# Two DMA queues for the first block's loads, and an earlier place for tile 3's statistics, in a transformer layer kernel

## The chip, the cores and the metric

The kernel runs on one core of a Trainium2 chip. Its time is the device time in microseconds (us) of one execution; the time before is the median of four runs. The core has a matrix engine (TensorE, PE in the profile), a vector engine (VectorE, DVE), an engine for activation functions (ScalarE, ACT), a general one (GpSimd, POOL) and one that mostly issues transfers (SyncE, SP). All data comes from and goes to the chip's main memory by DMA.

## The reference

A transformer layer on 2048 tokens with 1024 features: x plus attention of the normalised x, then that plus a dense part of its own normalised value.

```python
def _layernorm(x, axis=-1, eps=1e-5):
    m = jnp.mean(x, axis=axis, keepdims=True)
    v = jnp.var(x, axis=axis, keepdims=True)
    return (x - m) / jnp.sqrt(v + eps)

# attention: 32 heads of 32, each token sees itself and the 255 tokens before it
qkv = (x @ wqkv).reshape(B, S, 3, H, Dh).transpose(2, 0, 3, 1, 4)
scores = jnp.einsum("bhqd,bhkd->bhqk", q, k) * (Dh ** -0.5)
p = softmax(where(mask, scores, -1e9))
o = jnp.einsum("bhqk,bhkd->bhqd", p, v).transpose(0, 2, 1, 3).reshape(B, S, D) @ wo

h = x + attention(_layernorm(x))
h2 = h + silu(_layernorm(h) @ w1) @ w2      # w1: 1024 x 3584, w2: 3584 x 1024
```

All inputs and the output are bfloat16.

## The kernel before

The tokens are cut into four blocks of 512, each into four tiles of 128 tokens (one per partition). For each block the kernel normalises the tiles, turns them so that features lie on the partitions (`lnT_b`), and multiplies them by wqkv: V for each tile and column half (`v_group`, eight matmuls over kt, the eight slices of 128 features), then Q and K (`qk_group`, line 250). The attention of a block runs between the matmuls of the next one. Then come the output projection and the dense part, also matmul after matmul. All instructions of an engine run in the order in which they are written in the source; nothing is rearranged.

The change lies in the opening: the loads of block 0, lines 151 to 157, and the treatment of its four tiles, lines 495 to 541. There the order is written out by hand so that PE can start early:

- SP issues all loads, one behind the other: x tile 0 (x0), x1, the left half of wqkv's V columns in four quarters of 256 KB (two kt slices each), x2, the right half of V in two pieces of 512 KB, x3, and the first 512 columns of Q (1 MB). The other Q and K columns are issued only after the transposes of the three tiles below. The completion of transfers is counted on eight semaphores used in turn, and an issue that reuses one waits until its earlier transfer has landed.
- Tiles 0 and 1 are not normalised before they are multiplied, only centred: `mean_first` takes their means (ACT, lines 459 and 462; DVE, 460 and 461), `center` subtracts them (DVE, 468 and 470), and `turn_first` turns them on PE (line 218), with a copy out of PSUM on ACT or DVE (line 219). `v_group(0, 0, 0)` and `v_group(0, 1, 0)` multiply them, and `scaled` multiplies the results by the reciprocal standard deviation, which comes later from `var_first` and `root_first` on ACT (lines 487 and 490) and `ln_recip` on DVE (line 212).
- ACT's queue starts with the load of its function table and a dummy activation (line 149), then L459 for tile 0 and L462 for tile 1, then the copies of tile 0's turns.
- Tile 2 gets its statistics on DVE (`ln_stats`, lines 174 and 182), its root on ACT (`ln_root`, line 209), its reciprocal and its normalisation on DVE (`ln_norm`, line 202). It is turned on PE between the matmuls of the right V half of tiles 0 and 1 (line 525); ACT copies the four pieces.
- Tile 3 gets the same statistics, root and normalisation, and is turned by a DMA transpose (`ln_transpose`, line 206) from SP. `norm_first` (line 493) normalises tiles 0 and 1 fully for Q and K; they too are turned by DMA transposes, behind tile 3's.
- PE then multiplies tile 2 and tile 3 by both V halves (lines 537 to 541), and the Q and K groups follow.

On DVE, the order after tile 2's normalisation is: `norm_first(0)`, tile 3's statistics, `norm_first(1)`, tile 3's reciprocal and normalisation. On ACT, tile 3's root stands behind all four copies of tile 2's turns; behind it are the two evictions of the right V half of tiles 0 and 1 (line 532).

Of the kernel before, what the change touches and what calls it, by code (L numbers as in the profile page):

```python
# [44 lines left out]
def kernel(  # L45
# [10 lines left out]
    nc = tc.nc  # L56
# [3 lines left out]
    S, D = x2d.shape  # L60
# [34 lines left out]
    def view(region, off, *dims):  # L95
        n = 1
        for d in dims:
            n *= d
        ap = region[:, off:off + n]
        if len(dims) == 2:  # L100
            return ap.rearrange("p (a b) -> p a b", b=dims[1])
        if len(dims) == 3:
            return ap.rearrange("p (a b c) -> p a b c", b=dims[1], c=dims[2])
        return ap
# [5 lines left out]
    x_ring = [view(r_o, i * 1024, 1024) for i in range(8)]  # L110
# [17 lines left out]
    wqkv_v = A_wqkv.rearrange("(kt p) n -> p kt n", p=P)  # L128
# [5 lines left out]
    def load_x(b, j, queue=nc.sync):  # L134
        queue.dma_start(out=x_ring[(b % 2) * 4 + j], in_=x2d[(b * 4 + j) * P:(b * 4 + j + 1) * P, :])

    def load_wqkv(c0, parts=1):
        dst = wqk[:, :, c0:c0 + 512] if c0 < 2 * D else wv[:, :, c0 - 2 * D:c0 - 2 * D + 512]
        n = KT // parts
        for k in range(0, KT, n):  # L140
            nc.sync.dma_start(out=dst[:, k:k + n, :], in_=wqkv_v[:, k:k + n, c0:c0 + 512])

    warm = view(r_e, 0, P)
    nc.vector.memset(warm, 0.0)
# [4 lines left out]
    nc.scalar.activation(out=dummy[:], in_=eps[:], func=ACT.Sqrt)  # L149

    load_x(0, 0)
    load_x(0, 1)
    load_wqkv(2 * D, 4)
    load_x(0, 2)
    load_wqkv(2 * D + 512, 2)
    load_x(0, 3)
    load_wqkv(0)

    ident = const.tile([P, P], BF16, name="ident")
# [13 lines left out]
    def ln_half(xt, stats, c):  # L173
        nc.vector.bn_stats(out=stats[:, c, :], in_=xt[:, c * 512:(c + 1) * 512])

    def ln_stats(xt, st, j, half_done=None):
        stats = half_done
        if stats is None:
            stats = small.tile([P, 2, 6], F32, name="ln_st", tag="ln_st")
            ln_half(xt, stats, 0)  # L180
        ln_half(xt, stats, 1)
        nc.vector.bn_aggr(out=st[:, j, :], in_=stats[:])
# [18 lines left out]
    def ln_norm(xt, st, rs, j):  # L201
        nc.vector.tensor_scalar(out=xt, in0=xt, scalar1=st[:, j, 0:1], scalar2=rs[:, j:j + 1],
                                op0=ALU.subtract, op1=ALU.mult)
# [4 lines left out]
    def ln_root(st, rs, j):  # L208
        nc.scalar.activation(out=rs[:, j:j + 1], in_=st[:, j, 1:2], func=ACT.Sqrt, bias=eps[:], scale=1.0)
# [4 lines left out]
    def turn_first(j, h, src, copy):  # L214

        for i in range(2):
            kt = h * 2 + i
            nc.tensor.transpose(out=tp_ps[h][:, i * P:(i + 1) * P], in_=src[:, kt * P:(kt + 1) * P], identity=ident[:])
        copy(out=lnT_b[0][:, h * 2:(h + 1) * 2, j * P:(j + 1) * P],
             in_=tp_ps[h][:, 0:256].rearrange("p (k q) -> p k q", q=P))  # L220

    def ln_tiles(tag):
        st = small.tile([P, 4, 2], F32, name=f"st_{tag}", tag=f"st_{tag}")
        rs = small.tile([P, 4], F32, name=f"rs_{tag}", tag=f"rs_{tag}")
        return st, rs
# [9 lines left out]
    def v_group(b, j, c, copy, between=None):  # L235
        acc = next_acc()
        for kt in range(KT):
            if between:
                between(kt)
            nc.tensor.matmul(acc, lhsT=lnT_b[b % 2][:, kt, j * P:(j + 1) * P], rhs=wv[:, kt, c * 512:(c + 1) * 512],  # L240
                             start=(kt == 0), stop=(kt == KT - 1))
        copy(out=v[:, b * 4 + j, c * 16:(c + 1) * 16, 0:DH], in_=acc.rearrange("p (h d) -> p h d", d=DH))
# [207 lines left out]
    st, rs = ln_tiles("a")  # L450
# [41 lines left out]
    def norm_first(j):  # L492
        nc.vector.tensor_scalar(out=x_ring[j], in0=x_ring[j], scalar1=mean[:, j + 2:j + 3], scalar2=rs[:, j:j + 1], op0=ALU.add, op1=ALU.mult)
# [18 lines left out]
    ln_recip(rs, 1)  # L512
    ln_recip(rs, 2)
    ln_norm(x_ring[2], st, rs, 2)
    norm_first(0)
    v_group(0, 1, 0, hold)
    scaled(0)
    scaled(1)
# [1 line left out]
    for k in range(0, KT, 4):  # L520
        for j in range(2):
            for kt in range(k, k + 4):
                if k and j:
                    turn_first(2, kt - k, x_ring[2], act)
                nc.tensor.matmul(pair[j], lhsT=lnT_b[0][:, kt, j * P:(j + 1) * P], rhs=wv[:, kt, 512:1024], start=(kt == 0), stop=(kt == KT - 1))  # L525
    ln_stats(x_ring[3], st, 3)
    ln_root(st, rs, 3)
    norm_first(1)
    ln_recip(rs, 3)
    ln_norm(x_ring[3], st, rs, 3)  # L530
# [43 lines left out]
    for g0 in range(0, G, 4):  # L574
        for w in range(2):
            for g in range(g0, g0 + 4):
                qk_group(0, w, g, dve if g % 2 else act)
                n = g0 * 2 + w * 4 + g % 4
# [181 lines left out]
```

## Time and profile before

| | |
|---|---|
| Runs | 692.54, 694.46, 694.34, 692.54 us |
| Median | 693.44 us |
| Profiled execution | 692.29 us, of which the span from the first to the last instruction is 690.5 us |
| PE busy | 685.8 us, 99% of the span |
| DVE, ACT, POOL busy | 290.0, 244.4, 160.4 us |
| Bytes moved | 61.48 MB, 89 GB/s in the mean over the span |
| Granted PE clock | 1.0 |

The profile follows one execution. A line of the timeline gives the start of an instruction (in us from the span's start), its length, its engine, its source line, what it writes and reads, and in brackets how long the engine had been idle and what ended that. The names are those of memory regions: r_o holds the x tiles, r_w the weights of Q, K and V and the turned tiles, tp, acc and o_ps are PSUM banks. PE's matmuls overlap by a part of their shown length, so the distance between two starts is what one costs. PEld is the loading of PE's weights, SPq the issuing of transfers by SP.

### The profile page before, as it was taken

The numbers are of one execution on the slowest core, as the hardware profiler recorded it, in microseconds if no ns is written. First come the engines' busy times: TensorE is split into PE (matmuls) and PEld (weight loads), VectorE is DVE, ScalarE is ACT, GpSimd is POOL, SyncE is SP. The second block draws the span as 40 slices with busy tenths as digits, with TensorE's granted clock in tenths as the row PEclk, the third lists the DMA queues.
The fourth block names the chain that finished last, engine by engine and source line by source line (L and its number), as shares of the span: only waits on it lengthen the run. The fifth ranks groups of instructions, "written<-read, shape, count | busy, mean of one in ns | idle before, by whom it ended". The sixth has DMA issues, their size and how long they took to land.

```text
span 690.5 us, 14241 instructions
## 1 busy us (share of the span) xinstructions
PE 685.8 (99%) x6011; PEld 331.3 (48%) x6011; DVE 290.0 (42%) x613; ACT 244.4 (35%) x464; POOL 160.4 (23%) x295
## 2 busy tenths in 40 slices
PE   9999999999999999999999999999999999999998
PEld 4444555555555555544444444444444444444445
DVE  5167646744444449533316133343133251333111
ACT  7226666666676666421310033300133100233000
POOL 1007666566666656500000000000000000000000
PEclk9999999999999999999999999999999999999999
DMA  7833141136240889971023310022300123100110
GB/s 246 286 51 82 40 97 44 26 64 184 72 131 17 246 231 285 220 267 52 11 85 111 87 39 0 1 91 70 85 0 1 21 92 94 39 1 1 30 39 24
DMA packets 78640, 61.48 MB, mean 89 GB/s; under 512 B 52464, under 2 KB 62704, under 8 KB 78576
## 3 DMA queue, kind: packets, MB, share of 16 engines
q1 hardware_dynamic: 78576, 60.57, 31.3%
q8 instruction: 47, 0.77, 0.5%
q14 instruction: 17, 0.14, 0.1%
HBM read 39.85 MB, written 8.39 MB: 70 GB/s over the span
## 4 chain that ended last, share of the span: by engine, by line
PE 98%; DMA 1%; ACT 0%; SPq 0%; DVE 0%; issue 0%
PE hacc L670 19%; PE hacc L707 18%; PE acc L250 17%; PE acc L707 11%; PE acc L670 9%; PE acc L271 7%; PE acc L240 7%; PE o_ps L383 5%; PE sc L303 3%; PE hacc L271 2%; PE sc L355 1%; DMA r_w<-in_A_wqkv_dram 1%; PE sc L329 1%; PE o_ps L240 1%; DMA r_w<-r_o 0%; PE o_ps L525 0%
## 5 line engine op out<-in xcount | busy, mean ns | idle before, releaser
L373 POOL TENSOR_SCALAR_AFFINE_SELECT r_e<-r_e 128x512 bf16<-128x512 bf16 (+1 forms) x288 | 157.4, 561 | 125.9 <-ACT r_e L363 61.9
L707 PEld LDWEIGHTS <-r_a 128*128 128x128 bf16 x952 | 90.9, 98 | 103.0
L670 PEld LDWEIGHTS <-r_w 128*128 128x128 bf16 x896 | 87.4, 98 | 105.0
L707 PE MATMUL hacc<-r_a 128*128 128x512 bf16 (+2 forms) x616 | 122.5, 360 | 0.0
L670 PE MATMUL hacc<-r_e,r_w 128*128 128x512 bf16 x456 | 100.9, 379 | 0.0
L315 ACT ACTIVATE r_e<-sc 128x768 bf16<-128x768 f32 x96 | 78.2, 814 | 48.0 <-PE sc L303 44.8
L679 ACT ACTIVATE r_n<-hacc 128x512 f32<-128x512 f32 x30 | 17.9, 597 | 178.9 <-PE hacc L670 178.9
L707 PE MATMUL acc<-r_a 128*128 128x512 bf16 x336 | 74.0, 379 | 0.0
L250 PEld LDWEIGHTS <-r_w 128*128 128x128 bf16 x512 | 44.2, 97 | 46.1 <-issue 1.0
L250 PE MATMUL acc<-r_t,r_w 128*128 128x512 bf16 x256 | 63.4, 379 | 0.0
L252 DVE CAST r_a<-acc 128x512 bf16<-128x512 f32 x56 | 38.6, 690 | 55.3 <-PE acc L250 55.0
L250 PE MATMUL acc<-r_w 128*128 128x512 bf16 x256 | 59.9, 379 | 0.0
L383 PEld LDWEIGHTS <-r_e 128*128 128x128 bf16 x1440 | 47.4, 96 | 17.9
L271 PE MATMUL acc<-r_o,r_a 128*128 128x512 bf16 x208 | 51.9, 379 | 0.0
L670 PE MATMUL acc<-r_e,r_w 128*128 128x512 bf16 x216 | 49.1, 379 | 0.0
L383 PE MATMUL o_ps<-r_a,r_e 128*128 128x33 bf16 x1440 | 48.1, 178 | 0.0
L722 DVE SCALAR_TENSOR_TENSOR r_t<-hacc,r_t 128x512 bf16<-128x512 f32 (+2 forms) x22 | 14.0, 635 | 57.0 <-PE hacc L707 57.0
L316 ACT ACTIVATE r_e<-sc 128x256 bf16<-128x256 f32 x96 | 37.6, 392 | 0.0
L722 DVE SCALAR_TENSOR_TENSOR r_t<-acc,r_t 128x512 bf16<-128x512 f32 x12 | 8.3, 691 | 64.2 <-PE acc L707 64.2
L680 DVE SCALAR_TENSOR_TENSOR r_a<-r_n,hacc 128x512 bf16<-128x512 f32 x30 | 20.6, 688 | 33.0 <-ACT r_n L679 33.0
L670 PE MATMUL hacc<-r_a,r_w 128*128 128x512 bf16 x144 | 32.9, 379 | 0.0
L271 PEld LDWEIGHTS <-r_a 128*128 128x128 bf16 x256 | 21.8, 97 | 22.3
(100 smaller groups left out, 540.3 us busy)
## 6 DMA issues: line engine op xcount, KB each, us to landing
r_w<-in_B_w_dram SPq DMA_DIRECT2D x8, 896.0 KB, 5.2
r_a<-in_B_w_dram SPq DMA_DIRECT2D x7, 1024.0 KB, 7.5
r_o<-in_A_x_dram SPq DMA_DIRECT2D x16, 256.0 KB, 4.1
r_w<-in_A_wqkv_dram SPq DMA_DIRECT2D x4, 1024.0 KB, 8.8
h_dram<-r_t SPq DMA_DIRECT2D x16, 256.0 KB, 3.1
r_t<-h_dram SPq DMA_DIRECT2D x16, 256.0 KB, 2.8
out_dram<-r_t SPq DMA_DIRECT2D x31, 128.0 KB, 1.7
r_e<-h_dram SPq DMA_DIRECT2D x3, 1024.0 KB, 5.6
```

The lines of the kernel that those rows point to most:

```text
L240: nc.tensor.matmul(acc, lhsT=lnT_b[b % 2][:, kt, j * P:(j + 1) * P], rhs=wv[:, kt, c * 512:(c + 1) * 512], start=(kt == 0), stop=(kt == KT ...
L250: nc.tensor.matmul(acc, lhsT=wqk[:, kt, col0:col0 + P], rhs=lnT_b[b % 2][:, kt, :], start=(kt == 0), stop=(kt == KT - 1))
L252: copy(out=(qT, kT)[which][b][:, g, :], in_=acc)
L271: nc.tensor.matmul(acc, lhsT=qT[b][:, g, j * P:(j + 1) * P], rhs=wo[:, g, c * 512:(c + 1) * 512], start=(g == 0), stop=(g == G - 1))
L303: nc.tensor.matmul(sc[hh // 2][half * 64:half * 64 + 64, hh % 2, col:col + qb - qa], lhsT=kT[t // 4][r0:r0 + DH, g, k0:k0 + 64], rhs=qT[b] ...
L315: nc.scalar.activation(out=tri[:, :, :, 64:256], in_=both, func=ACT.Exp, scale=scale)
L316: nc.scalar.activation(out=e[:, 1024:1280].rearrange("p (h q) -> p h q", q=P), in_=bank[:, :, 192:320], func=ACT.Exp, scale=scale)
L373: nc.gpsimd.affine_select(out=dst, in_=src, pattern=[[0, n] for n in dst.shape[1:-1]] + [[sgn, P]], compare_op=ALU.is_ge if upper else ALU ...
L383: nc.tensor.matmul(o_ps[pair][:, qt * 2 + hh, 0:VW], lhsT=chunk_of(i, bank, piece, pair, hh), rhs=v[:, b * 4 + kt, g * 4 + pair * 2 + hh, ...
L670: nc.tensor.matmul(acc, lhsT=w1[:, kt, ft * P:(ft + 1) * P], rhs=ln2T[b][:, kt, :], start=(kt == 0), stop=(kt == KT - 1))
L707: nc.tensor.matmul(acc[:, 0:c1 - c0], lhsT=gT[:, ft, j * P:(j + 1) * P], rhs=w2[ft // 4][:, ft % 4, c0:c1], start=(ft == 0), stop=(ft == F ...
L722: nc.vector.scalar_tensor_tensor(out=t_out[j % 2][:, c0:c1], in0=acc[:, 0:c1 - c0], scalar=0.5, in1=t_in[j % 2][:, c0:c1], op0=ALU.mult, o ...
```

## The change

The loads of block 0 are shared between two queues. x0, quarters 1 and 3 of the left V half, and everything behind them stay on SP; x1 and quarters 2 and 4 are issued by ACT, behind the dummy activation and ahead of L459. `load_wqkv` gets a list of queues, which its pieces take in turn.

In the treatment of the tiles, `norm_first(0)` moves from behind tile 2's normalisation to behind tile 3's statistics, just ahead of `norm_first(1)`. The statistics and the root of tile 3 are written inside the loop over the right V half, behind the first turn of tile 2. On ACT this puts tile 3's root behind the first of the four copies instead of behind the last.

```diff
-    def load_wqkv(c0, parts=1):
+    def load_wqkv(c0, parts=1, queues=(nc.sync,)):
...
         for k in range(0, KT, n):
-            nc.sync.dma_start(out=dst[:, k:k + n, :], in_=wqkv_v[:, k:k + n, c0:c0 + 512])
+            queues[k // n % len(queues)].dma_start(out=dst[:, k:k + n, :], in_=wqkv_v[:, k:k + n, c0:c0 + 512])
...
     load_x(0, 0)
-    load_x(0, 1)
-    load_wqkv(2 * D, 4)
+    load_x(0, 1, nc.scalar)
+    load_wqkv(2 * D, 4, (nc.sync, nc.scalar))
     load_x(0, 2)
     load_wqkv(2 * D + 512, 2)
     load_x(0, 3)
...
     ln_norm(x_ring[2], st, rs, 2)
-    norm_first(0)
     v_group(0, 1, 0, hold)
     scaled(0)
     scaled(1)
...
             for kt in range(k, k + 4):
                 if k and j:
                     turn_first(2, kt - k, x_ring[2], act)
+                    if kt == k:
+                        ln_stats(x_ring[3], st, 3)
+                        ln_root(st, rs, 3)
                 nc.tensor.matmul(pair[j], lhsT=lnT_b[0][:, kt, j * P:(j + 1) * P], rhs=wv[:, kt, 512:1024], start=(kt == 0), stop=(kt == KT - 1))
-    ln_stats(x_ring[3], st, 3)
-    ln_root(st, rs, 3)
+    norm_first(0)
     norm_first(1)
     ln_recip(rs, 3)
     ln_norm(x_ring[3], st, rs, 3)
```

## The prediction

> **What bounds the kernel now.** The page comes first: its busy lines, then its chain.
>
> ```profile
> span 690.5 us, 14241 instructions
> ...
> PE 685.8 (99%) x6011; PEld 331.3 (48%) x6011; DVE 290.0 (42%) x613; ACT 244.4 (35%) x464; POOL 160.4 (23%) x295
> ...
> PE 98%; DMA 1%; ACT 0%; SPq 0%; DVE 0%; issue 0%
> ```
>
> TensorE (PE) holds 98% of the chain. The change touches only block 0's opening, so what matters is when PE, working without a pause from then on, starts its last delayed stretch. The chain of waits, asked for the first 50 us, names that place (start, length, what):
>
> ```profile
> 1.73 0.43 SPq L141
> ...
> 2.20 4.51 DMA r_w<-in_A_wqkv_dram
> ...
> 6.75 0.38 PE acc L240
> ...
> 8.90 1.73 PE o_ps L240 x8
> ...
> 13.37 1.35 ACT r_w L219 x4
> 14.72 0.20 ACT rs_a L209
> ...
> 15.15 0.56 DVE r_o L202
> ...
> 15.72 2.84 DMA r_w<-r_o
> ...
> 18.61 1.90 PE o_ps L240 x8
> ...
> 22.23 27.63 PE acc L250 x128
> ```
>
> Two things are late: V quarter 2 (landing 6.71), and the transpose of tile 3, which PE's group at 18.61 waits for. The timeline of PE, and below it that of DVE, shows by how much (start, length, instruction; in brackets the idle time before and what ended it):
>
> ```profile
> 16.09 1.89 PE L240 MATMUL o_ps<-r_w 128*128 128x512 bf16 x8
> 18.61 1.90 PE L240 MATMUL o_ps<-r_w 128*128 128x512 bf16 x8 [0.63 <-DMA r_w<-r_o]
> ```
>
> ```profile
> 11.29 0.55 DVE L202 TENSOR_SCALAR r_o<-r_o,st_a,rs_a 128x1024 bf16<-128x1024 bf16 x1
> 11.76 0.54 DVE L493 TENSOR_SCALAR r_o<-r_o,mean,rs_a 128x1024 bf16<-128x1024 bf16 x1
> 12.21 1.28 DVE L174 BATCH_NORM_STATS2 ln_st<-r_o 128x6 f32<-128x512 bf16 x2
> ...
> 14.95 0.16 DVE L212 RECIPROCAL rs_a<-rs_a 128x1 f32<-128x1 f32 x1 [0.80 <-ACT rs_a L209]
> ```
>
> The group of 16.09 is free for its successor after 8 x 0.216 (1.73 / 8 in the chain), at 17.82. PE idles 0.79 there. This is all that an earlier tile 3 alone can win, and all that a later PE can lose for nothing.
>
> **When the loads land.** From the DMA view in narrow windows, issue start plus time to landing: x0 0.81 + 2.8 = 3.6; x1 1.26 + 2.8 = 4.1; V quarters 1 to 4: 5.8, 6.7, 7.4, 8.0; x2 3.73 + 4.9 = 8.6; second V half 10.2 and 11.5; x3 as in the row below, 5.27 + 6.9 = 12.2. So tile 3's statistics at 12.21 start on its landing, and the matmul of kt = 6 (timeline: 8.08) on quarter 4's.
>
> ```profile
> r_o<-in_A_x_dram SPq DMA_DIRECT2D x1, 256.0 KB, 6.9
> ```
>
> ```profile
> 5.00:6.00 1.00, 0.85 (x7) 0.52 (x8) 1.00 (x5) 1.00 (x4) 0.00 (x0) 1.00 0.91 282
> ...
> 11.00:12.00 1.00, 1.00 (x7) 0.41 (x5) 0.87 (x3) 1.00 (x3) 0.00 (x0) 1.00 1.06 382
> ```
>
> The two rows of stages (last columns DMA share and GB/s) say that the 16 DMA engines are full from the start on, so all transfers ahead of x3, the same 2.75 MB as before, take as long in two queues as in one.
>
> **Part 1, two queues.** Removed from SP: three issues of 0.43 to 0.51 each. They cover nothing late, since transfers wait in line rather than for SP. Added on ACT, behind the table load (0.80 to 2.08) and the dummy activation (2.10): three issues. No row shows an issue on ACT; SP's rows give 0.40 as the lower and 0.84 (x3's) as the upper end, so 1.2 to 2.5 together. I take 0.45 each, as nearly all SP rows have, so ACT is free at 2.2 + 1.35 = 3.55. ACT's first statistic (L459) waits for x0 until 3.58 anyway: cost nothing, but up to 1.1 at the upper end.
>
> SP now holds its later issues for other landings: x3's for quarter 1's (5.8), the first wqk load's for quarter 3's. Both cost nothing while the 1.25 MB ahead of them is on its way until 11.5; without that cover each costs its delay.
>
> x1 is issued at 2.2 instead of 1.26. Its landing is bounded by 2.2 + 2.8 = 5.0 (x0's and x1's time in an empty line) and 2.2 + 4.9 = 7.1 (x2's, five transfers ahead). With equal shares x1 runs beside quarter 1, and both are done when the same bytes were done before, up to 5.8; I take 5.4. ACT then runs L462 from 5.4 instead of 4.34, and the two copies (L219) behind it 1.06 later, so kt = 0 starts near 6.97, not 5.91.
>
> Quarter 2 runs beside quarter 3, so it lands with it at 7.4 instead of 6.7. Quarter 4 runs beside x2: 8.6 to 8.7 if they share equally; if x2's rows, twice as long, take two thirds, half of quarter 4 is left when x2 is done (about 8.2) and goes at half speed, 2 x 0.35 more: about 9.1 including landing. So kt = 6, which could start at 8.08, is late by d = 0.7 to 1.1. The late kt = 0 is hidden in this: from 6.97, four matmuls and two pairs of transposes (0.22 and 0.11 each) and one copy of 0.37 bring kt = 4 near 8.0, kt = 6 near 8.7. I take d = 0.9.
>
> d below zero is possible too: if ACT's queue is given its turn first, quarters 2 and 4 come as early as they could. Its upper end is x1 at 7.1: kt = 0 then starts at 8.6, d = 2.6.
>
> The Trainium skill ("DMA: Bandwidth & Descriptors", section "Issuing engines are not separate DMA queues") speaks against a gain: queues of different engines end in the same 16 DMA engines, and several issuers save issue time only. By it the sum would hold no faster loading at all; by the row of 5 to 6 us, which at 282 GB/s is below the later 382, a little room is left, and rival 1 prices it.
>
> **Part 2, the order on DVE and ACT.** norm_first(0) (0.45, start to start 11.76 to 12.21) moves behind tile 3's statistics. This frees DVE at 11.76, but x3 lands at 12.2: no gain where it left. It returns before the reciprocal: +0.45. ACT's root of tile 3 (L209) moves from behind four copies to behind the first. It waits for the statistics there, and three copies, then the two scaled evictions, queue behind it; PE's group of 14.36 reads these copies from kt = 2 on. The root ends near 14.0; the copies follow at 14.4, 14.7 and 15.1, each ahead of its reader (14.8, 15.2, 15.7): cost nothing, unless x3 is over 0.4 late.
>
> The 0.80 that DVE idled before the reciprocal goes. Statistics to end of norm_first(1) was 12.21 to 14.15, 1.94; plus 0.45 moved, plus 0.20 and 0.57 for reciprocal and norm: the transpose is issued at s + 3.16, where s is the start of the statistics. With s = 12.21 this is 15.37, 0.35 sooner than 15.72. But DVE reaches the statistics at 11.76 + d, since tile 1's copies and tile 2's statistics run behind PE.
>
> **The sum.** The end moves by the larger of two: PE, d - 0.79; tile 3, max(-0.35, d - 0.45 - 0.35) = max(-0.35, d - 0.80). For d = 0.9 this is +0.11. On the profiled execution: 692.29 (span 690.5 and 1.8 outside it) becomes 692.4. The median of the runs, 693.44, stands 1.15 above; the same shift gives 693.5. The order of the transposes and all work from 22.23 on stay, and PE has no idle there for a shift to enter.
>
> **A second cost, told apart.** The warm-up matmuls step by 0.425 (weight loads at 1.46, 1.88, 2.31 in the timeline), later ones by 0.216; after two short waits PE keeps the faster step. The Trainium skill ("TensorE: Matmul & The Clock Gate", Part 1) has the full clock granted after a busy window of about 3.4 us whose phase is not the kernel's; estimated from that page, one more window at half clock would add 1.7, where the rows above charge an early wait of PE only with its own length. No row here shows such a loss.
>
> **Rivals.** Rival 1, faster: a second queue fills the gaps of 4 to 6 us (293 and 282 GB/s against about 375 later). That is 2 x (375 - 288) / 375 = 0.46 earlier for x3 and the quarters. With the order's 0.35, tile 3 comes 0.81 sooner and PE's idle is used up: 692.6. For: DMA share 0.91 there. Against: the engines are full anyway.
>
> Rival 2, slower: ACT's queue starts late and then gets the lesser share. x1 lands at 7.1, ACT's statistic holds the copies behind it, and d = 2.6: +1.8, 695.3. With issues of 0.84 on ACT it is 1.1 more: 696.4. It decides from d = 0.8 on, and every us beyond is lost. For: x1 is issued 0.9 later and quarters 2 and 4 now share with x2, which nobody needs before 9.2. Against: the quarters were in line already behind x1.
>
> Rival 3, the loading changes nothing that PE sees, only the order on ACT and DVE counts: -0.35, 693.1.
>
> **How the numbers follow.** Forecast 0.45, rival 1 0.18, rival 2 0.25, rival 3 0.12. 0.3% is 2.08 us, about what a measurement of this kernel can tell from no change. The four times before lie in two pairs, 692.54 twice and 694.34 and 694.46, so a median can move by 1 either way without the change. Faster by over 2.08 takes more than rival 1: its gain, the lower pair, and early waits that I can't see: 0.13. Slower by over 2.08 is rival 2 at or above its centre, and the forecast on the upper pair with d over 1.9: 0.27. Same: 0.60. The range's low end is the lower pair less 0.35 and 0.79, 691.4; its high end is rival 2's upper price, 696.4. The forecast's own range is 692.4 to 694.6, one us around it.
>
> **What would show it.** Right: x1 landing 5.0 to 5.8, quarters 2 and 4 near 7.4 and 8.7 to 9.1, kt = 6 near 9; x3 still near 12.2; DVE without idle before the reciprocal of tile 3; its transpose issued at 15.6 to 15.9; PE's group of tile 3 at 18.5 to 18.9 with almost no idle before it. Wrong: x3 landing before 11.8 (rival 1), kt = 0 after 8 or PE at tile 3 after 20 (rival 2), a matmul step of 0.43 after 6 us, or a stretch behind 22 us that is longer than before.

## The result, and the profile after

The changed kernel takes 691.66 us (median of 30 runs); the kernel before, over 48 runs, 692.69. The ratio is 0.9984 with a 95% interval of 0.9979 to 0.9989: about 1.1 us faster, a small gain but clear of the noise. (Ratio and interval are taken from all runs, so the ratio differs a little from the quotient of the medians.) The forecast of 693.5, no change with a slight loss, had the sign wrong; its range held the time.

The page of the profiled execution (691.60) first: its span, its busy line and the queues.

```profile
span 689.9 us, 14241 instructions
...
PE 686.1 (99%) x6011; PEld 331.7 (48%) x6011; DVE 289.9 (42%) x613; ACT 244.2 (35%) x464; POOL 160.9 (23%) x295
...
q1 hardware_dynamic: 77888, 59.78, 31.1%
...
q10 hardware_dynamic: 688, 0.79, 0.3%
```

The span is 0.6 shorter. ACT's queue is q10; its 0.79 MB are x1 and two quarters. The chain of waits for the first 50 us (start, length, what):

```profile
0.81 2.87 DMA r_o<-in_A_x_dram
...
3.70 0.70 DVE ln_half L174
...
5.16 0.65 PE tp L218 x4
5.81 0.43 PE o_ps L167 x2
6.24 0.43 PE acc L240
...
9.11 1.73 PE o_ps L240 x8
...
14.74 1.73 PE acc L240 x8
16.46 3.45 PE o_ps L240 x16
19.92 1.73 PE acc L240 x8
21.64 27.63 PE acc L250 x128
```

Neither a V quarter nor a transpose stands in it any more. After x0's landing and the first statistics, PE alone makes up the chain from 5.16 on; tile 3's group is part of one run of 16 matmuls from 16.46. The long stretch of Q and K, 27.63 us in both kernels, starts at 21.64 instead of 22.23. These 0.59 are nearly the whole difference of the two spans. The timeline of ACT's issues, and below it DVE around tile 3, show where they come from.

```profile
0.80 1.28 ACT L149 ACT_TABLE_LOAD   x1 [0.80 <-PEq L745]
...
1.06 0.39 ACTq L135 DMA_DIRECT2D r_o<-in_A_x_dram  x1
...
1.49 0.96 ACTq L141 DMA_DIRECT2D r_w<-in_A_wqkv_dram  x2
...
2.09 0.20 ACT L149 ACTIVATE dummy<-eps 128x1 f32<-128x1 f32 x1
```

```profile
11.97 1.28 DVE L174 BATCH_NORM_STATS2 ln_st<-r_o 128x6 f32<-128x512 bf16 x2
13.28 0.21 DVE L182 BATCH_NORM_AGGREGATE st_a<-ln_st 128x2 f32<-128x12 f32 x1
13.41 0.95 DVE L493 TENSOR_SCALAR r_o<-r_o,mean,rs_a 128x1024 bf16<-128x1024 bf16 x2
14.27 0.15 DVE L212 RECIPROCAL rs_a<-rs_a 128x1 f32<-128x1 f32 x1
```

ACT issues x1 at 1.06, while its table load is still running and a full microsecond ahead of the dummy activation that stands before the issue in the program. So x1 is issued 0.2 earlier than on SP, not 0.9 later: "behind the dummy activation" holds for the order of the program, not for the time. The second thing is the rate of the loads, in the stages (last columns: DMA share, GB/s), first the stage of 4 to 5 us before the change, then two stages after it, and x3's row in the DMA view:

```profile
4.00:5.00 1.00, 0.96 (x3) 0.15 (x1) 0.85 (x4) 0.97 (x3) 0.00 (x0) 1.00 0.91 293
```

```profile
4.00:5.00 1.00, 1.00 (x3) 0.15 (x1) 0.85 (x3) 0.97 (x3) 0.00 (x0) 1.00 1.05 363
5.00:6.00 1.00, 0.92 (x7) 0.47 (x6) 1.00 (x6) 1.00 (x4) 0.00 (x0) 1.00 1.07 376
```

```profile
r_o<-in_A_x_dram SPq DMA_DIRECT2D x1, 256.0 KB, 6.2
```

Before, the two stages had 293 and 282 GB/s. x3 is issued at 4.97 and lands at 11.2 instead of 12.2, though the same bytes go ahead of it.

### The profile page after: what moved, and what is told of

Same layout as the page of the kernel before. It is cut to its first block, busy times and chain, and to the rows that moved or that the text cites. A ratio compares the mean times of both kernels' runs of the same rounds, so it can differ in the third digit from the quotient of the medians.

```text
span 689.9 us, 14241 instructions
## 1 busy us (share of the span) xinstructions
PE 686.1 (99%) x6011; PEld 331.7 (48%) x6011; DVE 289.9 (42%) x613; ACT 244.2 (35%) x464; POOL 160.9 (23%) x295
## 4 chain that ended last, share of the span: by engine, by line
PE 99%; DMA 0%; DVE 0%; issue 0%; DVEq 0%
PE hacc L671 19%; PE hacc L708 18%; PE acc L250 17%; PE acc L708 11%; PE acc L671 9%; PE acc L240 7%; PE acc L271 7%; PE o_ps L383 5%; PE sc L303 3%; PE hacc L271 2%; PE sc L355 1%; PE o_ps L240 1%; PE sc L329 1%; DMA r_o<-in_A_x_dram 0%; PE tp L218 0%; PE acc L527 0%
## 5 line engine op out<-in xcount | busy, mean ns | idle before, releaser
L671 PE MATMUL hacc<-r_a,r_w 128*128 128x512 bf16 x144 | 32.9, 379 | 0.0
```

The costliest lines, as they stand in the source:

```text
L671: nc.tensor.matmul(acc, lhsT=w1[:, kt, ft * P:(ft + 1) * P], rhs=ln2T[b][:, kt, :], start=(kt == 0), stop=(kt == KT - 1))
```

## The experiments

Ratios are against the kernel before on the same chip, where its median was 692.39 to 692.69; "Q starts" is the start of the long Q and K stretch in the chain of waits (or the end of the wait ahead of it), the place where everything in the opening is settled.

| Kernel | Ratio (95%) | Median us | x3 lands | Q starts |
|---|---|---|---|---|
| before, two profiles | 1 | 692.69 (48 runs) | 12.2, 12.3 | 22.23, 23.13 |
| changed, three profiles | 0.9984 (0.9979 to 0.9989) | 691.66 (30 runs) | 11.2, 11.3, 11.6 | 21.64, 22.13, 21.50 |
| e1, only the queues | 0.9992 (0.9983 to 1.0001) | 692.29 | 11.5 | 22.46 |
| e2, only the order | 0.9993 (0.9984 to 1.0002) | 692.24 | 12.7 | 22.35 |
| e3, all quarters on ACT | 1.0012 (1.0003 to 1.0021) | 693.48 | 11.9 | 23.47 |
| e4, x0 in two halves | 1.0024 (1.0013 to 1.0034) | 695.06 | 12.5 | 24.66 |
| e5, one queue, two halves of V | 1.0008 (0.9997 to 1.0018) | 692.78 | 12.1 | 22.16 |
| e6, ACT's issues late | 1.0091 (1.0077 to 1.0104) | 699.04 | 12.5 | 29.64 |
| e7, one filler less | 0.9986 (0.9977 to 0.9995) | 691.55 | 11.8 | 21.41 |
| e8, tile 0's transpose first | 0.9986 (0.9977 to 0.9995) | 691.79 | 11.7 | 22.27 |
| e9, weight loads wait | 0.9998 (0.9989 to 1.0007) | 692.24 | 11.8 | 22.14 |

**Each half alone.** e1 takes only the load part of the change, e2 only the order:

```diff
 e1: the order of before, and
-    load_x(0, 1)
-    load_wqkv(2 * D, 4)
+    load_x(0, 1, nc.scalar)
+    load_wqkv(2 * D, 4, (nc.sync, nc.scalar))
 e2: the order of the change, with the two lines above as before
```

> Only the loads are shared between the two queues; the order on DVE and ACT is that of before. Theory A (the loads land 1.0 sooner because the second queue fills gaps of the DMA engines, but tile 3's old place in the order hides it): x3 lands near 11.2, rate of 4 to 6 us above 350 GB/s, PE begins its groups without a wait for a quarter, but tile 3's root stands behind four copies, which end near 14.9, so its transpose is issued near 15.8 as before and PE idles 0.5 to 0.6 before tile 3; time -0.1 us against before (ratio 0.9998). Theory B (what counts is that PE no longer waits for quarters 2 and 4, the order is idle): -0.8 to -1.1, ratio 0.9985.

> Only the order on DVE and ACT is changed; all loads stay on SP. Theory A: x3 still lands at 12.2 and bounds the statistics; the transpose is issued 0.35 sooner, at 15.4, and PE's idle before tile 3 shrinks to about 0.4; time -0.35 us (ratio 0.9995), and the 4 to 6 us stages stay near 290 GB/s with single engines up to 1 us late in quarters 1 to 3. Theory B: no change of time. A rival on the gap: it was an accident of the one profiled execution; then x3 lands before 11.7 here too.

Each gives 0.3 to 0.6 us (0.33 and 0.38 by the medians against 692.62 on that chip, 0.55 and 0.48 by the ratios), with an interval that reaches no change. By the ratios the two add up to 1.03, nearly the 1.1 of the whole change, so the times don't show that the halves need each other; nor do they tell theory A from theory B in e1. The chain of e1, and then DVE's timeline of e2, say what each still waits for:

```profile
13.59 1.35 ACT r_w L219 x4
14.95 0.20 ACT rs_a L209
...
15.95 2.84 DMA r_w<-r_o
...
18.84 1.90 PE o_ps L240 x8
```

```profile
12.77 1.29 DVE L174 BATCH_NORM_STATS2 ln_st<-r_o 128x6 f32<-128x512 bf16 x2 [0.73 <-DMA r_o<-in_A_x_dram]
```

In e1, x3 is there at 11.5, but tile 3's root stands behind four copies, so the transpose is issued at 15.95 and PE idles 0.79 (its group before is free at 16.32 + 1.73 = 18.05). In e2 the order is ready and DVE idles 0.73 for x3, which lands 0.6 later than in before; so the transpose is issued at 15.85, not at the 15.4 that was expected. In these two profiles each half waits for what the other removes, as theory A had it. One detail failed: in e1, PE also waits until 8.3 for quarter 4. In both profiles Q starts later than in before (22.46 and 22.35 against 22.23), so the gain in their times isn't located.

**Does the matching matter?** e3 puts x0 and x1 on SP and all four quarters on ACT.

```diff
-    load_x(0, 1, nc.scalar)
-    load_wqkv(2 * D, 4, (nc.sync, nc.scalar))
+    load_x(0, 1)
+    load_wqkv(2 * D, 4, (nc.scalar,))
```

> As the changed kernel, but x0 and x1 stay on SP and all four quarters go on ACT's queue. Theory A (any second queue fills the gaps, the matching of the order is idle): x3 lands at 11.0 to 11.4, the rate of 4 to 6 us is above 350 GB/s, quarter 4 lands before 8.1; ratio within 0.0004 of the changed kernel's 0.9984. Rival (the matching order matters): quarter 4 lands after 8.3 since it shares with x2 and the second V half, PE waits at kt = 6, ratio 0.9990 or more.

The rival is right: slower than before by 0.8. PE waits 1.21 for quarter 4, which lands at 10.1 (timeline of PE):

```profile
10.12 0.38 PE L240 MATMUL acc<-r_w 128*128 128x512 bf16 x1 [1.21 <-DMA r_w<-in_A_wqkv_dram]
```

The rate is high here too (372 and 366 GB/s in the same stages): faster loading alone is no gain when a piece that PE needs comes late. ACT's fourth issue had to wait until 3.46 for the reuse of x0's completion semaphore; its bytes then moved beside those that SP had issued before. How much either adds was not tried.

**How much early ACT issues matter.** e6 builds what the forecast had assumed, and more: ACT's issues stand behind L459.

```diff
 (mean_first)
         nc.scalar.activation(..., accum_out=mean[:, 0:1])      # L459, waits for x0
+        load_x(0, 1, nc.scalar)
+        load_wqkv(2 * D, 4, (None, nc.scalar))                 # quarters 2 and 4
```

> As the changed kernel, but ACT's three issues stand behind the first statistic (L459), which waits for x0: x1 is issued near 3.8 instead of 1.06. This builds what the forecast had assumed, a late second queue. By the forecast's rule: x1 lands near 6.8, kt = 0 starts near 8.4, quarter 4 lands near 10, d = 2.0 to 2.5, so +1.2 to +1.7 us against before (ratio 1.0017 to 1.0025); with the clock falling back to half during PE's waits, as in the run with x0 in halves, another +1.5 (1.004). Rival (how early ACT issues does not matter, two queues are what counts): ratio 0.9990 or less.

It costs 6.3 us, far more than either expectation. The DMA view of 4 to 6 us shows a single queue, and the DMA row of x1 (issued at 3.54, so landed at 10.15) the result; the chain gives the same length:

```profile
q1 hardware_dynamic: 422, 0.51, 91.5%
```

```profile
3.54 6.61 DMA r_o<-in_A_x_dram
```

In the changed kernel both queues move bytes there (58.7% and 47.3% of the engines' time). In e6, ACT's queue moves nothing before 6, and has 5.8% from 6 to 7: what SP had issued earlier goes first. Nearly equal shares, which the forecast took, come at once where both queues start together; in e6 they come only from 8 on (46.9% for ACT's queue from 8 to 9, 58.6% for SP's). A part of the loss is PE's clock, granted at 0.50 from 8 to 16: from kt = 0 to the end of the next group of eight matmuls PE needs 7.1 us (11.70 to 18.83 in the chain), against 4.6 in the changed kernel (6.24 to 10.84).

**The landing of x0.** e4 loads x0 in two column halves, one on each queue; x1 follows on ACT.

```diff
-    load_x(0, 0)
+    nc.sync.dma_start(out=x_ring[0][:, 0:512], in_=x2d[0:P, 0:512])
+    nc.scalar.dma_start(out=x_ring[0][:, 512:1024], in_=x2d[0:P, 512:1024])
     load_x(0, 1, nc.scalar)
```

> As the changed kernel, but x0 is loaded in two column halves, one on each queue, ahead of all else. Theory A (in the changed kernel nothing but x0's landing and what follows it bounds PE, which never waits after 5.2): x0 lands 0.2 to 0.4 sooner, everything up to tile 3 moves with it; ratio 0.9980. Rival (the start is bound by PE's slow early clock, so earlier work is done at half speed): landing sooner, time as the changed kernel's, 0.9984.

Both expectations fail. The first turn starts 0.3 sooner (4.87), but x1 now lands at 5.2, ACT's statistic of tile 1 waits for it, and the copies of tile 0 wait behind that: kt = 0 starts at 6.76. Quarter 2 lands at 8.4. During these waits the clock drops (stages; the column before DMA share is the granted clock):

```profile
7.00:8.00 1.00, 0.48 (x4) 0.20 (x3) 0.42 (x3) 0.37 (x1) 0.00 (x0) 1.00 1.02 328
8.00:9.00 1.00, 0.56 (x3) 0.29 (x3) 0.00 (x0) 0.00 (x0) 0.00 (x0) 0.74 1.07 370
9.00:10.00 1.00, 1.00 (x7) 0.45 (x5) 0.00 (x0) 0.74 (x2) 0.00 (x0) 0.50 1.08 379
```

In the chain the matmuls of this stretch take 0.43 instead of 0.22. That is the loss which the prediction had told apart.

**One queue, larger pieces.** e5 keeps all loads on SP and cuts the left V half in two.

```diff
-    load_wqkv(2 * D, 4)
+    load_wqkv(2 * D, 2)          # with the order of the change
```

> All loads on SP, the left V half in two pieces of 512 KB instead of four quarters; order on DVE and ACT as in the changed kernel. Theory A (with one queue single DMA engines fall behind by 0.5 to 1 us wherever a transfer of 256 KB follows another, and never catch up): with fewer seams the last engine is late by less, x3 lands at 11.4 to 11.8, ratio 0.9988 to 0.9993 (kt = 0 waits for a half, landing near 6.5, which takes 0.3 back). Rival (one queue loses time whatever the size of its pieces): x3 lands at 12.2 or later, ratio 0.9995 or more.

x3 lands at 12.1, near the rival's 12.2 and about as late as with quarters. The second of the two pieces lands at 8.1 and PE waits for it. The rate is another matter (stages of e5):

```profile
4.00:5.00 1.00, 1.00 (x3) 0.15 (x1) 0.85 (x4) 0.97 (x3) 0.00 (x0) 1.00 1.04 360
5.00:6.00 1.00, 0.91 (x7) 0.44 (x7) 1.00 (x6) 1.00 (x4) 0.00 (x0) 1.00 1.01 331
```

One queue with larger pieces fills most of the gap of 4 to 6 us, and still brings x3 no sooner. A transfer has landed when the last of the 16 DMA engines has finished its part, and the trace's completion records show when each did. The first engine finished x3 at 10.8 in e5, 10.7 in the changed kernel and 11.2 in before; the last at 12.1, 11.2 and 12.2. So e5 has the rate but not the landing: some of its engines fall behind, as the expectations say of single ones. In the first profile of before, 15 of the 16 engines had finished quarter 1 at 4.9 and one at 5.9, and by quarter 3 the spread over the engines was 1.2 us. In the changed kernel's first profile the spread stays at 0.4 to 0.5 until quarter 3. In e7, with two queues, one engine is also 1.1 late, and x3 still lands at 11.8. Why an engine falls behind, and why two queues lose less by it, these runs don't show.

**Fillers and second profiles.** e7 leaves out one of the two short filler pairs. The runs called before_again, after_again and after_timed are the two kernels unchanged.

```diff
-    for i in range(2):
-        busy(2)
+    busy(2)
```

> As the changed kernel, but one of the two short filler matmul pairs that keep PE occupied before kt = 0 is left out (the fillers write nothing that is used). Theory A (PE bounds the opening from its first turn on, so what PE does there at half speed counts fully): kt = 0 starts 0.2 sooner, ratio 0.9981 to 0.9983. Rival (kt = 0 waits for ACT's copy, and less filling lifts PE's clock later): 0.9984 or more.

> The kernel before, for a second profile. If single engines fall behind at random in one queue, the engine that is late, and the landing of x3, differ from the first profile: x3 anywhere from 11.6 to 12.8, with a spread over the engines of about 1 us. If the gap were fixed, x3 lands at 12.2 again and quarter 1 lands at 5.8.

> The changed kernel, for a second profile. Theory A: x3 lands at 11.1 to 11.8 (three profiles with two queues so far), against 12.2 to 12.75 in four with one queue; stages of 4 to 6 us above 340 GB/s; PE reaches tile 3 without idle or with less than 0.2. If the first profile was lucky, x3 lands at 12 or later.

e7 is no different from the changed kernel. In its profile kt = 0 waited for quarter 1 until 6.2, so theory A is not tested there. The second profiles confirm x3's landing by queue: 12.1 to 12.7 in four with one queue, 11.2 to 11.9 in eight with two (the seven that follow the matching order, and e3). The other two with two queues, e4 and e6, have it at 12.5: a second queue alone does not bring it sooner. Quarter 4 is not safely sooner either: it lands at 7.6 to 8.6 in the seven, against 8.0 and 8.1 before. The second profiles also bring something else. Their Q stretches start late for a reason behind tile 3 (timeline of PE, before_again, then after_again):

```profile
23.13 2.10 PE L250 MATMUL acc<-r_w 128*128 128x512 bf16 x8 [0.83 <-DMA r_w<-r_o]
```

```profile
22.13 1.24 PE L250 MATMUL acc<-r_w 128*128 128x512 bf16 x5 [0.80 <-DMA r_w<-r_o]
```

The last of the three transposes, tile 1's, took 4.4 us there instead of 2.7, and the Q groups wait for it. Without that wait after_again would be the earliest of the changed kernel's three profiles, at 21.3.

**The slow last transpose.** e8 issues tile 0's transpose first; e9 holds the next weight loads back until the last transpose has landed.

```diff
 e8:
-    for j in (3, 0, 1):
+    for j in (0, 3, 1):
 e9:
+    fence = const.tile([P, 2], BF16, name="fence")
+    nc.sync.dma_start(out=fence[:], in_=lnT_b[0][:, KT - 1, P:P + 2])
     for c0 in (D, 512, D + 512):
         load_wqkv(c0)
```

> As the changed kernel, but SP issues the DMA transpose of tile 0 ahead of tile 3's (order 0, 3, 1 in place of 3, 0, 1); tile 0 is ready near 13.9, tile 3 near 15.0. Theory C (some executions lose 0.8 to 1 us because the last transpose runs beside the next weight load, as in the second profile of the kernel before, where it took 4.4 instead of 2.7): the last transpose is issued near 16.7 instead of 17.7 and lands near 19.5, two us before PE needs it; tile 3's is issued 0.2 to 0.3 later and lands near 18.2, so PE waits 0.1 to 0.2: median 691.6 to 691.9, and no execution above 692.3. Rival (those executions come from elsewhere): the same share, one in five, lies above 692.5.

> As the changed kernel, with one transfer of 512 bytes on SP behind the three transposes; it reads a corner of tile 1's turned data, so SP waits until the last transpose has landed (near 20.6) and issues the next weight loads behind it, 0.8 to 1.5 later than before (they are needed from 28 on, landing near 28; the transfer's result is not used). Theory C (the last transpose takes 4.4 instead of 2.7 in some executions, because the weight load behind it takes the DMA engines): the last transpose always lands near 20.6, no execution above 692.2, median 691.3 to 691.6; or +0.3 to +1 if the first of these loads now lands after PE needs it. Rival (the slow transpose is not caused by the load behind it): one execution in five above 692.4, as in the changed kernel.

> The changed kernel again, timed on the same chip as the kernel with the waiting loads, and a third profile of it. Ratio to before 0.998 to 0.999; two levels of time, near 691.6 and 692.5, the higher one where the last transpose takes 4.4 us. x3 lands at 11.1 to 11.8.

Neither beats the changed kernel, which on the same chip as e9 gave 691.46 (0.9987, 0.9979 to 0.9996) on two levels: seven of eleven runs at 691.33 to 691.49, three at 692.1 to 692.3. In e8, SP is busy with the issue of tile 0's transpose from 14.41 to 15.74, and tile 3's behind it is issued at 15.85 instead of 15.04; three of eleven runs still lie above 692.2. In e9 three of eleven lie 0.6 to 1.0 above the median, as without the wait, and in its profile the transposes took 3.1 to 3.4. So the load behind the transposes isn't shown to be the cause, and theory C is not supported.

The traces hold another candidate. In both profiles with the 4.4 us, a transfer of 16 KB that the profile lists as instructions (queue q8) starts while the last transpose is under way, at 19.6 in before_again and at 18.6 in after_again; then under 15 GB/s move from 20.4 to 21.7 and from 19.4 to 20.7. The DMA view of after_again from 17 to 19.5 has it:

```profile
q8 instruction: 1, 0.02, 3.9%
```

In the other twelve profiles it starts after the last transpose has landed, at 22.1 to 32.9, but for e8: there it starts at 19.6, when nearly all bytes of the transpose have moved. No run shifted this transfer, so it is not shown to be the cause. Nor is the slow transpose the only way to the upper level: the profiled execution of e8, at 692.24, belongs to it, and its transposes took 2.8. There PE waits for quarter 4 until 8.6 and again for tile 3.

## Why the prediction was wrong, step by step

**The rule of the sum held.** It said that the end moves by the larger of d - 0.79 (PE) and s + 3.16 - 15.72 (tile 3), d being the delay of kt = 6 and s the start of the statistics. The timeline of PE, before and then after, has the fillers, kt = 0 and kt = 6:

```profile
5.42 0.38 PE L167 MATMUL o_ps<-r_e 128*128 128x256 bf16 x2
5.91 0.38 PE L240 MATMUL acc<-r_w 128*128 128x512 bf16 x1
...
8.08 0.38 PE L240 MATMUL acc<-r_w 128*128 128x512 bf16 x1
```

```profile
5.60 0.63 PE L167 MATMUL o_ps<-r_e 128*128 128x256 bf16 x2
6.03 0.63 PE L240 MATMUL acc<-r_w 128*128 128x512 bf16 x1
...
8.29 0.38 PE L240 MATMUL acc<-r_w 128*128 128x512 bf16 x1
```

So d = 0.21, and s = 11.97. That gives -0.58 and -0.59; measured are -0.59 at the Q stretch and a transpose issued at 15.04, -0.68. In after_again and after_timed kt = 6 starts at 7.98 and 8.15, so the term of PE is -0.89 and -0.72; measured against 22.23 are -0.90, without the wait for tile 1's transpose, and -0.73. The inputs failed. The rule also divides the error of the forecast, +0.11, in this profile: d = 0.21 with x3 still at 12.2 gives -0.35, and the earlier x3 turns that into -0.58.

**First failing step: when ACT issues.** The prediction put the three issues behind the table load and the dummy, at 2.2. They ran from 1.06 to 2.45. With them, and with the higher rate, x1's landing was 4.3 (predicted 5.0 to 5.8), quarter 2's 5.7 (7.4), quarter 4's 7.6 (8.6 to 9.1), by issue plus time to landing. Quarter 4 had some luck in this profile: in e8, with the same loads, it landed at 8.6. Of each issue's length it was right: 0.39 to 0.5. The remaining d = 0.21 is not from loads, for PE waits for none; its slower step, 0.43 a matmul, lasted longer in this execution (the two fillers take 0.63 against 0.38 before, and kt = 0 takes 0.43 in the chain). The column of the granted clock reads 1.00 in both, so only the steps show this. In after_again, where kt = 0 takes 0.23, d is -0.10.

**Second failing step: "the engines are full".** It read the DMA share of 0.91 as full and forecast x3 at 12.2. The rows of 293 and 282 GB/s were a gap, which a second queue filled; e5 filled most of it in one queue, but with the last engine 1.4 us behind the first at x3. In the eight profiles with two queues and x3 at 11.2 to 11.9 these are 0.5 to 1.1 apart. What makes an engine late stays open. Issue time on SP can't explain it: quarters 2 to 4 and x2 were all issued by 4.2, a megabyte in line while the engines had gaps until 6. The Trainium skill ("DMA: Bandwidth & Descriptors", section "Issuing engines are not separate DMA queues") lets a second issuer save issue time only. The measurement differs: x3 came 1.0 sooner. Of this only 0.24 could be used, since DVE is free for the statistics at 11.97 and not before.

Two readings beside it were too firm: kt = 6 at 8.08 and the statistics at 12.21 show no wait in the profile before. PE and DVE had just ended the work ahead of them when quarter 4 and x3 landed.

**Rival 1 came nearest**: x3 0.46 earlier by its sum, 1.0 by the trace. Its price of 0.81 was near the 0.59 of the profile and the 1.1 of the runs. The pair of profiles shows less than the runs, in part because the profile of before, at 692.29, lies 0.4 below the median of its kernel. Without the wait for tile 1's transpose, the three profiles of the changed kernel start Q 0.74 before 22.23 in the mean, near the low end of the runs' interval (0.8 to 1.5). That wait moves single executions by 0.8 in both kernels; how often was not counted.

**Rival 2** described a real danger. With ACT's issues later still (3.54 instead of 2.2) it came out at 6.3, not 1.8 to 2.9: x1 landed at 10.15 and not at 7.1, and PE lost clock, which that price left aside. Its own case, issues at 2.2, was not built. The second cost that the prediction told apart, PE losing its clock in an early wait, did not come with the change, but did in e4 and e6: the granted clock of e4 was 0.74, then 0.50. The Trainium skill ("TensorE: Matmul & The Clock Gate", Part 1) has the clock fall to half after an idle window of about 3.4 us. The half agrees with these rows; but PE was not idle in e4, it was busy for 58%, 24% and 48% of the three microseconds from 5 to 8.

**Part 2 of the change was right in its mechanism**: the 0.80 of idle before the reciprocal is gone, and the copies behind the moved root were in time. Its size is not confirmed: e2 gave 0.4 to 0.5 where 0.35 was worked out, but with an interval that reaches no change, and in its profile x3 was late.

## What to carry to other kernels

A rate well under what the same transfers reach later is room, even at a DMA share near one (282 GB/s at 0.91 here, 382 at 1.06 later); take the later rate as the bound before calling loading fixed. But the rate is not the landing: e5 had the rate, and its last engine was as late as before. In these runs two loading queues paid when both started at once and each carried the pieces in the order of their use; one that started 2.5 us later, or carried all the urgent pieces, cost more than it gave. Before an earlier landing is priced, ask when its reader is free: of x3's 1.0 us, 0.24 was used. And where several things are late, either half of the change alone gave a third to a half of the gain here, too little to tell from nothing.

## What was not expected of the hardware

- ACT issued transfers from 1.06 on, during its table load (0.80 to 2.08) and before an activation that precedes them in the program ran (2.09).
- A queue that started behind a backlog moved nothing for over two microseconds: issued at 3.54, nothing before 6, landed at 10.15 (e6). Two that started together had 58.7% and 47.3% (the changed kernel, 4 to 6 us).
- The same DMA transpose of a tile took 2.7 us in some executions and 4.4 in others, at the same place of the same kernel. In both profiles with the 4.4, a transfer of instructions fell into it; that this is the cause is not shown.
